# Hand-written semaphores and a TensorE hardware loop in a decode attention kernel that streams 280 MB

## The chip, the cores and the metric

The kernel runs on 1 core of one Trainium2 chip. The metric is the device time of one execution in microseconds (us), median of several. The profile is one execution taken by the hardware profiler; its span is about 1.8 us shorter than the time.

## The reference

One decode step. Attention reads a long K and V cache (2 x 8 x 32768 x 128 each, bf16, 134 MB each); a small MLP gates the result.

```python
# Both parts get xn = layernorm(A_x) as their x.
B, Sq, D = 2, 1, 512
Hq, Hkv, Sk, Dh = 32, 8, 32768, 128
# A: attention with cached K and V; rep = Hq // Hkv = 4 query heads share one K/V head
q = (x @ wq) per head
scores = einsum("bhqd,bhkd->bhqk", q, k) * Dh ** -0.5
o = einsum("bhqk,bhkd->bhqd", softmax(scores), v)
s = o.reshape(B, Sq, Hq * Dh) @ wo
# B: with S = 1 its shifted part is zero, so it is x + gelu(layernorm(x) @ w3) @ w4
g = silu(B(xn))
return A_x + s * g          # xn = layernorm(A_x)
```

## The kernel before

There are 16 groups (2 batch rows x 8 K/V heads). A group loads 8.4 MB of K and 8.4 MB of V, each as one transfer over 128 partitions. VectorE transposes K in 16 pieces, TensorE makes the scores, ScalarE exponentiates, VectorE transposes the probabilities, TensorE multiplies with V. Everything is in tile pools, and a scheduling layer puts in the semaphores.

```python
pers  = ctx.enter_context(tc.tile_pool(name="pers", bufs=1))
rings = ctx.enter_context(tc.tile_pool(name="rings", bufs=1))
...
kbuf = rings.tile([128, 3 * SLOT], BF16, name="kbuf")     # SLOT: 32 KB per partition
vbuf = rings.tile([128, 2 * SLOT], BF16, name="vbuf")
...
def emit_k(m, h, first):
    ...
    for r in range(NR):                                   # NR = 8
        T = ktp.tile([128, W], I32, tag="T", name="T")
        nc.vector.transpose(out=T[...], in_=kt[:, r * W:(r + 1) * W]...)
        for nb in range(NB):
            for e in range(2):
                nc.tensor.matmul(sc[:, :], lhsT=z[...], rhs=Tb[:, nb, :, e], ...)
    # exp on ScalarE, transpose of the result on VectorE
...
for m in range(NG):                                       # NG = 16, written out
    eps = [emit_k(m, hs[0], True)]
    if not last:
        load_k(*groups[m + 1], (m + 1) % 2, 2 if m == NG - 2 else 1)
    eps.append(emit_k(m, hs[1], False))
    for i in range(NPART):
        emit_v(m, hs[i], i, eps[i])
    if not last:
        load_v(*groups[m + 1], 2 if m == NG - 2 else 1)
    if m == NG - 2:
        # wo, in three pieces, into the free part of kbuf
```

The tail after the last loads is a chain: the last half of V lands, 32 matmuls finish o, ScalarE copies it out, eight small matmuls reduce it (oT), VectorE normalizes and spreads it (on, xm, oX), 128 matmuls multiply with wo, two VectorE operations combine with the gate, and two small transfers write the output.

The softmax here doesn't subtract the row's maximum and nothing guards it: scores larger than these inputs give would overflow.

Of the kernel before, what the change touches and what calls it, by code (L numbers as in the profile page):

```python
# [8 lines left out]
F32 = mybir.dt.float32  # L9
BF16 = mybir.dt.bfloat16  # L10
ACT = mybir.ActivationFunctionType
ALU = mybir.AluOpType
AX = mybir.AxisListType

I32 = mybir.dt.int32

KPT = 128
# [4 lines left out]
EPS = 1e-5  # L22


@with_exitstack
def kernel(
# [14 lines left out]
    nc = tc.nc  # L41

# [19 lines left out]
    QP = 32 * (NQ - 1) + B  # L62

    pers = ctx.enter_context(tc.tile_pool(name="pers", bufs=1))
    rings = ctx.enter_context(tc.tile_pool(name="rings", bufs=1))
    ktp = ctx.enter_context(tc.tile_pool(name="ktp", bufs=T_BUFS))
    epp = ctx.enter_context(tc.tile_pool(name="epp", bufs=2))
    ptp = ctx.enter_context(tc.tile_pool(name="ptp", bufs=3))
    obp = ctx.enter_context(tc.tile_pool(name="obp", bufs=2))
    smp = ctx.enter_context(tc.tile_pool(name="smp", bufs=4))  # L70
    pro_ps = ctx.enter_context(tc.tile_pool(name="pro_ps", bufs=1, space=bass.MemoryType.PSUM))
    f_ps = ctx.enter_context(tc.tile_pool(name="f_ps", bufs=3, space=bass.MemoryType.PSUM))
    sc_ps = ctx.enter_context(tc.tile_pool(name="sc_ps", bufs=2, space=bass.MemoryType.PSUM))
    o_ps = ctx.enter_context(tc.tile_pool(name="o_ps", bufs=2, space=bass.MemoryType.PSUM))

    kbuf = rings.tile([128, 3 * SLOT], BF16, name="kbuf")
    vbuf = rings.tile([128, 2 * SLOT], BF16, name="vbuf")

    def row_view(cache, b, g):
        return cache[b, g, :, :].rearrange("(p t) d -> p (t d)", p=128)  # L80

    def load_k(b, g, base, parts=1):
        w = NPART * SLOT // parts
        src = row_view(A_k_cache, b, g)
        for c in range(parts):
            nc.sync.dma_start(
                out=kbuf[:, base * SLOT + c * w:base * SLOT + (c + 1) * w],
                in_=src[:, c * w:(c + 1) * w],
            )

    def load_v(b, g, parts=1):
        w = NPART * SLOT // parts
        src = row_view(A_v_cache, b, g)
        for c in range(parts):
            nc.sync.dma_start(out=vbuf[:, c * w:(c + 1) * w], in_=src[:, c * w:(c + 1) * w])  # L95


    x_bf = pers.tile([B, D], BF16)
    nc.scalar.dma_start(out=x_bf[:, :], in_=A_x[:, 0, :])
    wq_t = kbuf[:, 2 * SLOT:3 * SLOT]  # L100
    nc.sync.dma_start(  # L101
        out=wq_t[:, 0:DK * HD],
        in_=A_wq.rearrange("(p k) f -> p (k f)", k=DK),
    )

    x4_bf = pers.tile([128, QW], BF16)
    nc.gpsimd.memset(x4_bf[:, :], 0.0)
    for n in range(NQ):
        nc.gpsimd.dma_start(out=x4_bf[32 * n:32 * n + B, :], in_=A_x[:, 0, n * QW:(n + 1) * QW])
    groups = [(b, g) for b in range(B) for g in range(Hkv)]  # L110
    NG = len(groups)
    w34 = vbuf[:, 0:SLOT]
    W4O = DK * Fdim
    nc.sync.dma_start(out=w34[:, 0:W4O], in_=B_w3.rearrange("(p k) f -> p (k f)", k=DK))  # L114
    nc.sync.dma_start(out=w34[:, W4O:W4O + FK * D], in_=B_w4.rearrange("(p f) d -> p (f d)", f=FK))  # L115
    load_k(*groups[0], 0)


    ident = pers.tile([128, 128], BF16)
    make_identity(nc, ident[:, :])  # L120
    ones_f = pers.tile([128, 128], F32)
    nc.gpsimd.memset(ones_f[:, :], 1.0)


    sel = pers.tile([128, NB, 2, 4, 32], BF16)
    for j in range(4):
        nc.vector.tensor_copy(
            out=sel[:, :, :, j, :],
            in_=ident[:, :].rearrange("p (b w e) -> p b e w", b=NB, e=2),
        )  # L130

    sel_o = pers.tile([128, VT, rep], F32)
    nc.vector.tensor_reduce(
        out=sel_o[:, :, :],
        in_=ident[:, :].rearrange("p (j a t h) -> p a t h j", j=4, t=VT, h=rep)[:, 0, :, :, :],
        axis=AX.X, op=ALU.add,
    )
    sel_h = pers.tile([128, rep], F32)
    nc.vector.tensor_reduce(
        out=sel_h[:, :],  # L140
        in_=ident[:, :].rearrange("p (r h) -> p h r", h=rep),
        axis=AX.X, op=ALU.add,
    )

    sel_r = pers.tile([128, NQ, 4, 32], BF16)
    for j in range(4):
        nc.vector.tensor_copy(
            out=sel_r[:, :, j, :],
            in_=ident[:, :].rearrange("p (w r) -> p r w", r=NQ),
        )  # L150

    mask = pers.tile([128, NQ, rep], F32)
    for r in range(NQ):
        nc.vector.tensor_reduce(
            out=mask[:, r, :],
            in_=ident[:, :].rearrange("p (h w) -> p h w", h=rep),
            axis=AX.X, op=ALU.add,
        )

    zs = [pers.tile([128, NB, 2, ZC], BF16, name=f"z{i}") for i in range(2)]  # L160
    for z in zs:
        nc.gpsimd.memset(z[:, :, :, :], 0.0)


    xf = pers.tile([B, D], F32)
    nc.vector.tensor_copy(out=xf[:, :], in_=x_bf[:, :])

    def layernorm(dst, src, t):
        stats = pers.tile([B, nc.vector.BN_STATS_DIM], F32, name=f"stats_{t}")
        nc.vector.bn_stats(out=stats[:, :], in_=src[:, :])  # L170
        mv = pers.tile([B, nc.vector.BN_AGGR_DIM], F32, name=f"mv_{t}")
        nc.vector.bn_aggr(out=mv[:, :], in_=stats[:, :])
        rstd = pers.tile([B, 1], F32, name=f"rstd_{t}")
        nc.vector.tensor_scalar_add(out=rstd[:, :], in0=mv[:, 1:2], scalar1=EPS)
        nc.scalar.activation(out=rstd[:, :], in_=rstd[:, :], func=ACT.Sqrt)
        nc.vector.reciprocal(out=rstd[:, :], in_=rstd[:, :])
        nc.vector.tensor_scalar(
            out=dst[:, :], in0=src[:, :],
            scalar1=mv[:, 0:1], scalar2=rstd[:, 0:1],
            op0=ALU.subtract, op1=ALU.mult,  # L180
        )

    xn = pers.tile([B, D], F32)
    layernorm(xn, xf, "ln1")
    xn4 = pers.tile([128, QW], F32)
    nc.gpsimd.memset(xn4[:, :], 0.0)
    for n in range(NQ):
        nc.gpsimd.dma_start(out=xn4[32 * n:32 * n + B, :], in_=xn[:, n * QW:(n + 1) * QW])
    ln2 = pers.tile([B, D], F32)
    layernorm(ln2, xn, "ln2")  # L190
    xn_bf = pers.tile([B, D], BF16)
    nc.vector.tensor_copy(out=xn_bf[:, :], in_=xn[:, :])
    ln2_bf = pers.tile([B, D], BF16)
    nc.vector.tensor_copy(out=ln2_bf[:, :], in_=ln2[:, :])

    treg = pro_ps.tile([128, 2 * DK * B], BF16, tag="pro")
    for s, src in enumerate((xn_bf, ln2_bf)):
        for k in range(DK):
            c = (s * DK + k) * B
            nc.tensor.transpose(out=treg[:, c:c + B], in_=src[0:B, k::DK], identity=ident[0:B, 0:B])  # L200
    xT = pers.tile([128, 2 * DK, B], BF16)
    nc.vector.tensor_copy(out=xT[:, :, :], in_=treg[:, :].rearrange("p (k b) -> p k b", b=B))

    q_sb = pers.tile([128, B, Hq], BF16)

    oX = pers.tile([128, Hkv, NQ, B], BF16)
    g4 = pers.tile([128, QW], F32)
    x4 = pers.tile([128, QW], F32)
    nc.gpsimd.tensor_copy(out=x4[:, :], in_=x4_bf[:, :])

    wq3 = wq_t[:, 0:DK * HD].rearrange("p (k f) -> p k f", k=DK)
    qT_ps = pro_ps.tile([128, Hq * B], F32, tag="pro")
    for h in range(Hq):
        for k in range(DK):
            nc.tensor.matmul(  # L215
                qT_ps[:, h * B:(h + 1) * B],
                lhsT=wq3[:, k, h * Dh:(h + 1) * Dh],
                rhs=xT[:, k, :],
                start=(k == 0), stop=(k == DK - 1),
            )  # L220
    nc.vector.tensor_copy(out=q_sb[:, :, :], in_=qT_ps[:, :].rearrange("p (h b) -> p b h", b=B))

    qr_ps = pro_ps.tile([128, NB, 2, B * Hq], F32, tag="pro")
    for nb in range(NB):
        for e in range(2):
            nc.tensor.matmul(
                qr_ps[:, nb, e, :],
                lhsT=sel[:, nb, e, :, :].rearrange("p j w -> p (j w)"),
                rhs=q_sb[:, :, :].rearrange("p b h -> p (b h)"),
                start=True, stop=True,  # L230
            )
    qr = pers.tile([128, NB, 2, B, Hq], BF16)
    nc.vector.tensor_copy(  # L233
        out=qr[:, :, :, :, :].rearrange("p n e b h -> p (n e b h)"),
        in_=qr_ps[:, :, :, :].rearrange("p n e c -> p (n e c)"),
    )

    def emit_mlp():
        w3v = w34[:, 0:W4O].rearrange("p (k f) -> p k f", k=DK)
# [206 lines left out]
```

## Time and profile before

| | before |
|---|---|
| time, median (3 runs) | 660.86 us (660.72 to 660.88) |
| span of the profiled run | 658.9 us |
| bytes from HBM | 280.5 MB, 426 GB/s over the span |
| VectorE waiting for K | 150.5 us in 16 waits, 9.4 us per group |
| last half of V landed / last wo piece landed | 644.11 / 653.99 us |

The page of the kernel before, part 2: the TensorE clock that was granted and the mean busy share of the transfer engines (both in tenths of the full value), and their rate, in 40 slices of the span.

```profile
PEclk9999688786968968697886959878596877859896
DMA  9999999999999999999999999999999999999995
GB/s 367 451 426 442 435 446 439 410 443 426 439 438 435 430 435 422 447 434 423 442 427 442 438 419 434 443 434 443 414 423 446 443 442 443 410 427 428 431 421 224
```

The transfer engines are busy in 39 slices of 40. The last slice is the tail. Part 4 of the same page, the chain of work that ended last, by engine and by line, says the same in one line:

```profile
DMA 75%; DVE 14%; issue 7%; PE 3%; SPq 0%; ACT 0%; DVEq 0%
DMA kbuf<-in_A_k_cache_dram 69%; DVE T L303 14%; DMA kbuf<-in_A_wo_dram 6%; PE sc L311 2%; PE o L343 1%; PE s_ps L400 0%; ACT ep L320 0%; SPq L95 0%; DVE pt L322 0%; SPq L115 0%; SPq L392 0%; SPq L114 0%; SPq L101 0%; PE S L339 0%; DVE sg L408 0%
```

Part 5, two groups of instructions (busy time and mean ns of one, then idle time before them and what ended it):

```profile
L311 PE MATMUL sc<-T,z 128*128 128x512 bf16 x992 | 276.4, 421 | 206.3 <-DVE T L303 197.8
L303 DVE STREAM_TRANSPOSE T<-kbuf 128x1024 int32<-128x1024 int32 x256 | 291.5, 1205 | 150.5 <-DMA kbuf<-in_A_k_cache_dram 150.5
```

VectorE's transposes wait 150.5 us for K; each K load is what the group waits for, and compute has slack.

The trace also records the semaphore increments of each transfer (they are in the packed trace; no view prints them). There are sixteen per load, each with a time of its own. I read each as one of the sixteen transfer engines having landed its part; that is a reading, which the trace doesn't spell out. I call the distance from the first to the last of them the *lag* of the slowest engine. For the last half of V in the kernel before, in us after 639.54:

```
0.00 0.02 0.05 0.14 0.24 0.48 0.51 2.85 2.93 2.96 2.97 2.98 4.32 4.51 4.55 4.57
```

Which engine posted which is not in the trace. Compute starts when the sixteenth is in: it came at 644.11 us, and the first matmul of the half started at 644.15 us.

### The profile page before, as it was taken

To read this page: it belongs to the slowest core of one execution; us is meant where nothing else is said; L and a number is where in the kernel's file an instruction comes from. 1 tells how busy PE (TensorE), PEld (TensorE's weight loads), DVE (VectorE), ACT (ScalarE), POOL (GpSimd) and SP (SyncE) were. 2 spreads that over 40 slices of the span, in tenths; PEclk is the share of its full clock that TensorE was granted. 3 is DMA by queue.
4 is the path that set the end of the run, shared out by engine and by line. 5 is a ranking of instruction groups with operands and counts; after the bars stand their busy time and mean duration, and the time that the engine had idled before them with its cause. 6 is when DMAs were issued, how large, how long until landed. Compare 5 with 4: busy or idle time off the path is not lost.

```text
span 658.9 us, 6323 instructions
## 1 busy us (share of the span) xinstructions
PE 386.7 (59%) x2652; PEld 172.1 (26%) x2684; DVE 346.0 (53%) x442; ACT 50.3 (8%) x152; POOL 6.9 (1%) x20
## 2 busy tenths in 40 slices
PE   2338194673828557283764729377482946738764
PEld 2313132231313223131331313123131322313322
DVE  5147192754809265381935629183572918447560
ACT  1301001010100101000010100101010010100000
POOL 4000000000000000000000000000000000000000
PEclk9999688786968968697886959878596877859896
DMA  9999999999999999999999999999999999999995
GB/s 367 451 426 442 435 446 439 410 443 426 439 438 435 430 435 422 447 434 423 442 427 442 438 419 434 443 434 443 414 423 446 443 442 443 410 427 428 431 421 224
DMA packets 6704, 280.91 MB, mean 426 GB/s; under 512 B 906, under 2 KB 916, under 8 KB 1940
## 3 DMA queue, kind: packets, MB, share of 16 engines
q1 hardware_dynamic: 6408, 280.50, 98.6%
q8 instruction: 21, 0.34, 0.2%
q0 software_dynamic: 256, 0.01, 0.0%
q14 instruction: 7, 0.06, 0.0%
q10 hardware_dynamic: 12, 0.00, 0.0%
HBM read 280.50 MB, written 0.00 MB: 426 GB/s over the span
## 4 chain that ended last, share of the span: by engine, by line
DMA 75%; DVE 14%; issue 7%; PE 3%; SPq 0%; ACT 0%; DVEq 0%
DMA kbuf<-in_A_k_cache_dram 69%; DVE T L303 14%; DMA kbuf<-in_A_wo_dram 6%; PE sc L311 2%; PE o L343 1%; PE s_ps L400 0%; ACT ep L320 0%; SPq L95 0%; DVE pt L322 0%; SPq L115 0%; SPq L392 0%; SPq L114 0%; SPq L101 0%; PE S L339 0%; DVE sg L408 0%
## 5 line engine op out<-in xcount | busy, mean ns | idle before, releaser
L311 PE MATMUL sc<-T,z 128*128 128x512 bf16 x992 | 276.4, 421 | 206.3 <-DVE T L303 197.8
L303 DVE STREAM_TRANSPOSE T<-kbuf 128x1024 int32<-128x1024 int32 x256 | 291.5, 1205 | 150.5 <-DMA kbuf<-in_A_k_cache_dram 150.5
L311 PEld LDWEIGHTS <-z 128*128 128x128 bf16 x1024 | 105.7, 103 | 371.2 <-issue 278.7
L343 PE MATMUL o<-vbuf,pt 128*16 128x512 bf16 x1024 | 69.9, 434 | 3.2 <-DMA vbuf<-in_A_v_cache_dram 3.2
L320 ACT ACTIVATE ep<-sc 128x512 bf16<-128x512 f32 x32 | 19.1, 597 | 493.2 <-PE sc L311 451.2
L334 DVE MEMSET o<- 128x512 f32 x16 | 7.8, 485 | 69.3 <-ACT ob L352 68.3
L322 DVE STREAM_TRANSPOSE pt<-ep 128x512 bf16<-128x512 bf16 x32 | 22.6, 707 | 34.7 <-ACT ep L320 34.4
L343 PEld LDWEIGHTS <-pt 128*16 128x16 bf16 x1024 | 27.2, 99 | 37.9 <-issue 18.2
L339 PE MATMUL S<-sm,ones_f 128*128 128x4 f32 x64 | 10.7, 238 | 26.1 <-DVE sm L338 26.1
L355 PE MATMUL oT<-sel_o,ob 128*128 128x4 f32 x128 | 16.9, 255 | 11.1 <-ACT ob L352 11.1
L355 PEld LDWEIGHTS oT<-sel_o,ob 128*128 128x128 f32 x128 | 15.5, 191 | 19.3 <-ACT ob L352 19.3
L339 PEld LDWEIGHTS S<-sm,ones_f 128*128 128x128 f32 x64 | 10.7, 188 | 30.9 <-DVE sm L338 28.4
L352 ACT COPY ob<-o 128x512 f32<-128x512 f32 x16 | 9.4, 586 | 83.4 <-PE o L343 83.4
L362 DVE TENSOR_TENSOR on<-oT,rec 128x4 bf16<-128x4 f32 x16 | 2.6, 162 | 21.8 <-PE oT L355 21.8
L286 ACT COPY z<-qr 32x16 bf16<-32x16 bf16 x64 | 12.6, 198 | 11.5 <-DVE qr L233 10.9
L360 DVE RECIPROCAL rec<-S 128x4 f32<-128x4 f32 x16 | 2.9, 182 | 7.6 <-PE S L339 7.6
L365 PEld LDWEIGHTS <-sel_r 128*128 128x128 bf16 x64 | 5.2, 117 | 5.2 <-issue 5.2
L320 ACT ACTIVATION_READ_ACCUMULATOR ep<-sc 128x1 f32 x32 | 6.3, 198 | 0.2
L215 PE MATMUL qT_ps<-xT,kbuf 128*128 128x2 bf16 x128 | 3.6, 165 | 4.5 <-DMA kbuf<-in_A_wq_dram 4.5
L365 PE MATMUL xp<-on,sel_r 128*128 128x4 bf16 x64 | 3.8, 164 | 4.1 <-DVE on L362 4.1
L338 DVE TENSOR_SCALAR sm<-sel_h,rs 128x4 f32<-128x4 f32 x32 | 6.0, 188 | 0.0
L370 DVE TENSOR_TENSOR xm<-xp,mask 128x16 f32<-128x16 f32 x16 | 2.8, 174 | 5.3 <-PE xp L365 5.3
(64 smaller groups left out, 48.5 us busy)
## 6 DMA issues: line engine op xcount, KB each, us to landing
kbuf<-in_A_k_cache_dram SPq DMA_DIRECT2D x2, 4096.0 KB, 29.1
vbuf<-in_A_v_cache_dram SPq DMA_DIRECT2D x2, 4096.0 KB, 26.7
kbuf<-in_A_wq_dram SPq DMA_DIRECT2D x1, 4096.0 KB
vbuf<-in_B_w_dram SPq DMA_DIRECT2D x2, 1792.0 KB, 21.6
kbuf<-in_A_wo_dram SPq DMA_DIRECT2D x1, 2048.0 KB, 35.9
kbuf<-in_A_wo_dram SPq DMA_DIRECT2D x1, 1536.0 KB, 39.1
kbuf<-in_A_wo_dram SPq DMA_DIRECT2D x1, 512.0 KB
kbuf<-in_A_k_cache_dram SPq DMA_DIRECT2D x15, 29.4
```

The source lines that it names most:

```text
L286: nc.scalar.copy(out=z[32 * j:32 * j + 32, :, :, c:c + rep], in_=qr[32 * j:32 * j + 32, :, :, b, g * rep:(g + 1) * rep],)
L303: nc.vector.transpose(out=T[:, :].rearrange("p (b t k) -> p t b k", b=NB, t=RT), in_=kt[:, r * W:(r + 1) * W].rearrange("p (t b k) -> p t ...
L311: nc.tensor.matmul(sc[:, :], lhsT=z[:, nb, e, zc:zc + 128], rhs=Tb[:, nb, :, e], start=(r == 0 and nb == 0 and e == 0), stop=(r == NR - 1 ...
L320: nc.scalar.activation(out=ep[:, :], in_=sc[:, :], func=ACT.Exp, scale=inv_sqrt_dh, accum_out=rs[:, :])
L322: nc.vector.transpose(out=pt[:, :, :].rearrange("p r (t h) -> p t r h", h=rep), in_=ep[:, :].rearrange("p (t r h) -> p t r h", r=NR, h=rep),)
L334: nc.vector.memset(state["o"][:, :], 0.0)
L338: nc.vector.tensor_scalar_mul(out=sm[:, :], in0=sel_h[:, :], scalar1=rs[:, 0:1])
L339: nc.tensor.matmul(S[:, :], lhsT=ones_f[:, :], rhs=sm[:, :], start=(i == 0), stop=(i == NPART - 1))
L343: nc.tensor.matmul(o[32 * j:32 * j + VT * rep, :], lhsT=pt[:, r, a * VT * rep:(a + 1) * VT * rep], rhs=vt[:, u * VT:(u + 1) * VT, :].rearr ...
L352: nc.scalar.copy(out=ob[:, :], in_=o[:, :])
L355: nc.tensor.matmul(oT[:, :], lhsT=ob[:, t * Dh:(t + 1) * Dh], rhs=sel_o[:, t, :], start=(t == 0), stop=(t == VT - 1),)
L365: nc.tensor.matmul(xp[:, r, :], lhsT=sel_r[:, r, :, :].rearrange("p j w -> p (j w)"), rhs=on[:, :], start=True, stop=True,)
```

## The change

The intent: put everything in one hand-synchronized section, so that no scheduler waits are left, and turn 15 of TensorE's 16 groups into a hardware loop. The loop body is the same in each turn, so TensorE waits for a fixed value there instead of a growing count and then lowers the semaphore itself (a *take-down*, `take` below). The order of loads, the tile sizes and the arithmetic stay. The diff, cut to its core:

```diff
+def take(eng, sem, n=1):
+    eng.wait_ge(sem, n).then_inc(sem, -n)
...
-    pers = ctx.enter_context(tc.tile_pool(name="pers", bufs=1))
-    rings = ctx.enter_context(tc.tile_pool(name="rings", bufs=1))
-    # ... nine more pools ...
-    kbuf = rings.tile([128, 3 * SLOT], BF16, name="kbuf")
-    vbuf = rings.tile([128, 2 * SLOT], BF16, name="vbuf")
+    pers = ctx.enter_context(tc.tile_pool(name="pers", bufs=1))
+    psum = ctx.enter_context(tc.tile_pool(name="psum", bufs=1, space=bass.MemoryType.PSUM))
+    kbuf = pers.tile([128, 3 * SLOT], BF16, name="kbuf")     # now the first tile of the pool
+    vbuf = pers.tile([128, 2 * SLOT], BF16, name="vbuf")
+    Ts = [pers.tile([128, RT * NB * 32], I32, name=f"T{i}") for i in range(T_BUFS)]
...
+    with tc.tile_critical():
...
+        for m in range(1, NG):                       # SyncE
+            wait(sp, (p_t, NT * (m - 1) + NR)); load_k(m)
+            wait(sp, (p_o, m));                 load_v(m)
...
+        def scores():
+            take(pe, s_z)
+            for i in range(NPART):
+                for r in range(NR):
+                    take(pe, s_t)
+                    # four matmuls
+                    last_mm.then_inc(p_t.sem, 1)
...
+        with pe.Fori(0, last):
+            scores()
+            values(lambda h: take(pe, s_v, 16) if h == 0 else None)
+        scores()
+        values(lambda h: wait(pe, (d_vl[h], 16)))
```

VectorE, ScalarE and SyncE stay written out. Small things also moved: x is loaded by ScalarE's queue four times after a memset, eight small GpSimd transfers are gone, z has one buffer, and the reciprocal of the softmax sum now comes after the oT matmuls.

## The prediction

> **What bounds the kernel now.** Transfers do. The page gives a mean DMA share of 90% or more in 39 of 40 slices and 426 GB/s over the span; the chain of waits is 75% DMA. One group's 16.8 MB of K and V take 38.6 us (transfers of K land at 119.6, 158.2, 197.2 us). The compute of a group is shorter: VectorE transposes (1.2 us each, 16 per group) and TensorE leave VectorE idle for K 150.5 us in 16 waits (groups view), 9.4 us per group. Each K load is issued 29 us, each V load 32 us before landing, so the queue never runs empty. Only the start and the end are open: the first transfer is issued at 0.74 us, the last two pieces of wo land at 652.7 and 653.9 us, the span ends at 658.9 us.
>
> **A second-order effect that the change touches.** The trace shows the 16 engines' increments of each large transfer. They land within 0.6 us of each other at 10 us, but within 2.0 us at 60 us, 3.1 us at 310 us and 4.5 us at the last wo pieces, in steps of about 1.45 us: for the second wo piece seven engines within 0.5 us, then five at 2.8 to 3.0, four at 4.2 to 4.5. Meanwhile the queue of instruction fetches has 21 packets of 16 KiB (page, part 3), 0.9 us each. I read each fetch as delaying one DMA engine by about 1.45 us; the slowest engine, with three, sets every landing. [...] 21 blocks is about TensorE's unrolled stream (2652 matmuls, 2684 weight loads).
>
> **What the change does.** Same work, tiles, loads and order of loads. Removed: the scheduler's waits, one buffer of z, a third pt, 15 of 16 memsets of o (0.49 us each, off the path), eight small GpSimd transfers. Added: a few dozen waits, some 20 take-downs per group on TensorE, a loop-back branch; the first x loads wait for a memset and queue behind wq, so layer norm may come about 10 us later. In the profile of before the MLP ends at 25 us, the first K lands at 42 us, so V's first load, which waits for the MLP, still has time. None of this is on the path: about 9 us of slack per group absorbs it.
>
> TensorE's program shrinks to about 1,370 instructions, 5 to 6 blocks. If the loop body (about 300 instructions, 19 KB) stays resident, engine spread falls from 4.5 to about 1.5 to 2 us, and all late landings come 2 to 3.5 us earlier, V's last half included, so the tail moves whole. If each turn fetches its two or three pages again[...], there are 30 to 45 fetches, and the spread stays or grows by up to 3 us. I give residence 60%.
>
> **Prediction.** 658.3 us, 8 in 10 between 655.5 and 663. Faster by over 2%: 1%; within 2%: 96%; slower by over 2%: 3%.
>
> **What would show each step.** Instruction packets on the queue of TensorE: 5 to 7 (resident) or over 30. Spread of the 16 landings at the last wo piece: about 1.5 us or 4.5 and more. DMA rate in the middle unchanged (about 430 GB/s); VectorE still idle for K about 9 us per group; tail from last wo landing to end still about 5 us.
>
> **What would make it wrong.** x landing so late that the first V load comes after 40 us; a loop-back stall over 9 us; a costly entry or exit of the hand-made section; or transfers bounded by something shared, so that spread costs nothing (then within 1 us of before).

From the page before, as an estimate: 21 packets of 16 KiB on q8 for 2652 matmuls and 2684 weight loads are about 254 instructions per packet, or 64.5 bytes each, if q8 carries TensorE's program (a1 tests that). 1,370 instructions are then 5.4 packets. The forecast's sum: it came to 660.8 us less about 2.5 us for earlier landings, 658.3 us. The 60% for residence were my estimate.

## More of the kernel before

Part 3, the queues (packets, MB, share of the time of 16 engines):

```profile
q1 hardware_dynamic: 6408, 280.50, 98.6%
q8 instruction: 21, 0.34, 0.2%
...
q14 instruction: 7, 0.06, 0.0%
```

q1 carries the loads. q8 and q14 carry instructions: 21 packets of 16 KiB on q8 and, within the loads, six packets of 8 KiB on q14.

The tail of the kernel before in the timeline view (start us, duration us, engine, line, operation, output<-inputs, count, and in brackets the idle time before it and what ended it):

```profile
644.15 3.38 PE L343 MATMUL o<-vbuf,pt 128*16 128x512 bf16 x32 [3.18 <-DMA vbuf<-in_A_v_cache_dram]
...
647.58 0.59 ACT L352 COPY ob<-o 128x512 f32<-128x512 f32 x1 [9.74 <-PE o L343]
...
648.22 1.05 PE L355 MATMUL oT<-sel_o,ob 128*128 128x4 f32 x8 [0.69 <-ACT ob L352]
...
649.32 0.16 DVE L362 TENSOR_TENSOR on<-oT,rec 128x4 bf16<-128x4 f32 x1 [9.96 <-PE oT L355]
...
649.70 1.09 PE L400 MATMUL s_ps<-kbuf,oX 128*2 128x128 bf16 x64
...
650.01 0.17 DVE L372 TENSOR_REDUCE oX<-xm 128x4 bf16<-128x16 f32 x1
652.79 1.88 PE L400 MATMUL s_ps<-kbuf,oX 128*2 128x128 bf16 x64 [2.00 <-DMA kbuf<-in_A_wo_dram]
...
655.43 0.66 SPq L412 DMA_DIRECT2D out_dram<-out  x1
```

And the same stretch by windows (us of each engine's busy time, number of instructions, then granted clock, transfer share, GB/s):

```profile
644.00:648.00 4.00, 3.38 (x32) 1.03 (x31) 0.00 (x0) 0.42 (x1) 0.00 (x0) 0.60 1.04 426
648.00:652.00 4.00, 2.31 (x76) 2.06 (x77) 0.51 (x3) 0.17 (x1) 0.00 (x0) 0.83 0.71 288
652.00:656.00 4.00, 1.88 (x64) 1.58 (x63) 0.58 (x2) 0.00 (x0) 0.00 (x0) 0.50 0.14 55
```

Here the first 64 wo matmuls start at 649.70 us, before the last oX is done, and the others then wait for the second and third piece of wo (652.74 and 653.99 us), so the landing of wo ends the kernel.

## The result and the profile after

| | before | after |
|---|---|---|
| time, median (4 runs each) | 660.79 us | 661.22 us (660.88 to 661.54) |
| ratio | | 1.0006, 95% interval 0.9992 to 1.0020 |
| span of the profiled run | 658.9 us | 659.8 us |
| instruction packets on q8 | 21 | 5 |
| VectorE waiting for K | 150.5 us | 150.5 us |
| last half of V landed: first engine / last | 639.54 / 644.11 us | 640.80 / 644.96 us |
| last wo piece landed | 653.99 us | 654.98 us |

A ratio is the mean time of one kernel's runs over that of the other's of the same rounds, so it is not quite the ratio of the medians quoted. Executions over 1.5% slower than the fastest of the same kernel are left out of the means.

The page after, parts 2 and 3:

```profile
DMA  8999999999999999999999999999999999999994
GB/s 366 434 443 441 434 445 421 421 445 433 441 442 405 441 434 441 441 445 401 441 433 445 441 413 429 438 441 441 441 401 445 433 445 437 417 429 430 421 421 197
```

```profile
q1 hardware_dynamic: 6408, 280.50, 98.5%
q8 instruction: 5, 0.08, 0.1%
q14 instruction: 6, 0.05, 0.0%
```

The loop does what it was meant to do: q8 falls from 21 to 5 packets. The body, an estimated 300 instructions from counting the source, or 19 KB at 64.5 bytes each (the estimate from the page before, given beside the prediction), is fetched once and then stays for 15 turns: the packets start at 28.4, 35.4, 69.3, 641.1 and 653.7 us, none in between. Yet the loads don't end earlier. The chain view of after:

```profile
PE 1%; DVE 0%; issue 0%
PE bank L540 1%; DVE sg L547 0%; DVE out L549 0%; PE bank L519 0%; DVE xm L470 0%; DVE oX L473 0%
```

It stops after 12 pieces, at the first take-down. The groups say what happened to it:

```profile
L486 PE MATMUL bank<-T,z 128*128 128x512 bf16 x1024 | 283.1, 428 | 184.7 <-PEq L45 179.6
L449 DVE STREAM_TRANSPOSE T<-kbuf 128x1024 int32<-128x1024 int32 x256 | 290.6, 1206 | 150.5 <-DMA kbuf<-in_A_k_cache_dram 150.5
```

TensorE's waits are now put down to "PEq L45", its own sequencer at the helper `take`, which lowers the semaphore itself. The 1% is a limit of the view and no finding. VectorE still waits 150.5 us for K, so the middle of the kernel is bound as before. The tail of after:

```profile
645.00 3.59 PE L503 MATMUL bank<-vbuf,pt 128*16 128x512 bf16 x32 [5.08 <-DMA vbuf<-in_A_v_cache_dram]
...
648.65 0.59 ACT L431 COPY ob<-bank 128x512 f32<-128x512 f32 x1 [12.14 <-PE bank L503]
...
649.38 1.84 PE L513 MATMUL bank<-sel_o,ob 128*128 128x4 f32 x8 [0.78 <-PEq L45]
...
651.47 0.16 DVE L468 TENSOR_TENSOR on<-bank,rec 128x4 bf16<-128x4 f32 x1
...
652.27 0.17 DVE L473 TENSOR_REDUCE oX<-xm 128x4 bf16<-128x16 f32 x1
...
652.50 3.58 PE L540 MATMUL bank<-kbuf,oX 128*2 128x128 bf16 x128 [0.47 <-DVE oX L473]
...
656.77 0.65 SPq L553 DMA_DIRECT2D out_dram<-out  x1
```

```profile
644.00:648.00 4.00, 3.00 (x32) 0.98 (x32) 0.00 (x0) 0.00 (x0) 0.00 (x0) 0.50 1.02 407
648.00:652.00 4.00, 2.65 (x20) 1.97 (x12) 0.34 (x2) 0.59 (x1) 0.00 (x0) 0.50 0.78 310
652.00:656.00 4.00, 3.53 (x129) 3.29 (x128) 0.35 (x2) 0.00 (x0) 0.00 (x0) 0.50 0.06 22
```

Three things differ. The last half of V lands 0.85 us later; its first engine is 1.26 us later, of which 0.21 us were there from the start, since the first transfer is issued at 0.95 instead of 0.74 us. TensorE runs the rest at a granted clock of 0.50: the oT matmuls take 1.84 us instead of 1.05. The clock records show that it fell to 0.50 during the wait for V in both kernels, at 643.78 us before and 642.99 us after, but came back at 647.19 us before and not until 656.65 us after. The idle wait was 5.1 us after and 3.2 us before; that this decided it was not tested. And the hand-written section has one wait of its own here: all 128 wo matmuls wait for the last oX and run in one go from 652.50 to 656.08 us, where the first 64 used to start ahead of it. The output transfer is issued at 656.77 instead of 655.43 us. The close after the output's landing is some 0.5 us shorter, so that 0.9 us is left in these two spans.

The lag tells why the landing didn't profit. For four loads of the changed kernel, the five latest of the sixteen engines, in us after the first one:

```
first at 214.85   0.90 1.22 1.56 1.68 1.73
first at 234.21   0.89 1.54 1.65 1.71 2.16
first at 427.75   0.89 1.51 1.62 1.69 3.11
first at 601.93   0.88 1.49 1.59 1.65 4.12
```

One engine goes from 1.22 to 2.16 to 3.11 to 4.12 us while the others stand still. Its steps fall at the q14 packets of 232.5, 424.6 and 604.6 us. A packet at 47.7 us seems to have made the 1.22, which first shows in the next load. These are spaced by about 185 us; VectorE has an estimated 29 instructions per group in the built program, so 8 KiB (127 instructions at the same estimate of 64.5 bytes) last about 4.4 groups of 38.7 us, 170 us. So I took them for VectorE's program, all fetched by the same transfer engine. The fifth packet within the loads, at 188.0 us, moved another engine (to 0.90 us). The experiments test the reading.

### The profile page after: what moved, and what is told of

The parts are those of the page before. It is cut to its first block, busy times and chain, and to the rows that moved or that the text cites. A ratio compares the mean times of both kernels' runs of the same rounds, so it can differ in the third digit from the quotient of the medians.

```text
span 659.8 us, 6521 instructions
## 1 busy us (share of the span) xinstructions
PE 393.7 (60%) x2684; PEld 165.5 (25%) x2684; DVE 337.0 (51%) x428; ACT 50.3 (8%) x152; POOL 5.7 (1%) x18
## 5 line engine op out<-in xcount | busy, mean ns | idle before, releaser
L486 PE MATMUL bank<-T,z 128*128 128x512 bf16 x1024 | 283.1, 428 | 184.7 <-PEq L45 179.6
L449 DVE STREAM_TRANSPOSE T<-kbuf 128x1024 int32<-128x1024 int32 x256 | 290.6, 1206 | 150.5 <-DMA kbuf<-in_A_k_cache_dram 150.5
L486 PEld LDWEIGHTS bank<-T,z 128*128 128x128 bf16 x1024 | 99.3, 104 | 362.0 <-issue 283.6
L503 PE MATMUL bank<-vbuf,pt 128*16 128x512 bf16 x1024 | 68.2, 426 | 5.1 <-DMA vbuf<-in_A_v_cache_dram 5.1
L423 ACT ACTIVATE ep<-bank 128x512 bf16<-128x512 f32 x32 | 19.1, 598 | 482.2 <-PE bank L486 482.2
L503 PEld LDWEIGHTS bank<-vbuf,pt 128*16 128x16 bf16 x1024 | 26.4, 98 | 38.8 <-issue 12.6
L496 PE MATMUL bank<-sm,ones_f 128*128 128x4 f32 x64 | 9.4, 252 | 27.6 <-PEq L45 27.6
L513 PE MATMUL bank<-sel_o,ob 128*128 128x4 f32 x128 | 17.2, 258 | 12.5 <-PEq L45 12.5
L513 PEld LDWEIGHTS bank<-sel_o,ob 128*128 128x128 f32 x128 | 16.3, 199 | 20.5 <-issue 20.5
L496 PEld LDWEIGHTS bank<-sm,ones_f 128*128 128x128 f32 x64 | 8.5, 192 | 35.4 <-issue 35.4
L431 ACT COPY ob<-bank 128x512 f32<-128x512 f32 x16 | 9.4, 586 | 87.6 <-PE bank L503 87.6
```

What stands on the lines that cost most here:

```text
L423: act.activation(out=eps_[i][:, :], in_=sc[i][:, :], func=ACT.Exp, scale=inv_sqrt_dh, accum_out=rss[NPART * (m % 2) + i][:, :],)
L431: act.copy(out=ob[:, :], in_=o[:, :]).then_inc(s_ob, 1)
L449: dve.transpose(out=Ts[n % T_BUFS][:, :].rearrange("p (b t k) -> p t b k", b=NB, t=RT), in_=kt[:, r * W:(r + 1) * W].rearrange("p (t b k) ...
L486: last_mm = pe.matmul(sc[i][:, :], lhsT=z[:, nb, e, zc:zc + 128], rhs=Tb[:, nb, :, e], start=(r == 0 and nb == 0 and e == 0), stop=(r == N ...
L496: pe.matmul(S, lhsT=ones_f[:, :], rhs=sms[h][:, :], start=(h == 0), stop=(h == NPART - 1))
L503: last_mm = pe.matmul(o[32 * j:32 * j + VT * rep, :], lhsT=pts[h][:, r, a * VT * rep:(a + 1) * VT * rep], rhs=vt[:, u * VT:(u + 1) * VT, : ...
```

## The experiments

Theory L: a packet of instructions delays the one transfer engine that fetches it; the engine that lags most sets each landing; VectorE's packets all hit the same one. Rivals: only the bytes count (the engines share one limit), or the take-downs and waits cost time. From the first four runs came theory A: the start address of the K and V buffers sets the pace of all engines.

All runs gave right results. They came in three batches on three chips (a on chip 4, b on 6, c on 14), each with the kernel before beside it: 660.76, 660.79 and 660.84 us, so times of different batches can be compared to about 0.1 us. Times are medians of 5 runs; "V" is the last half of V in the profiled run; the pace is the mean time from one load of 8.4 MB to the next at which the first of the sixteen engines lands, over the 29 steps between 40 and 602 us.

| run | time us | ratio to before | packets: q8 in all / q14 within the loads | pace us | V: first, last, lag us |
|---|---|---|---|---|---|
| before | 660.8 | 1 | 21 / 6 | 19.328 | 639.54, 644.11, 4.57 |
| after, again (a0) | 661.20 | 1.0008 | 5 / 5 | 19.353 | 640.70, 644.83, 4.13 |
| a1 loop written out | 662.43 | 1.0020 | 22 / 5 | 19.354 | 640.67, 645.87, 5.20 |
| a2 more VectorE instructions | 664.49 | 1.0057 | 5 / 8 | 19.353 | 641.39, 647.73, 6.33 |
| a3 TensorE kept warm | 661.13 | 1.0006 | 5 / 5 | 19.352 | 640.59, 644.91, 4.31 |
| b1 buffers at multiples of 512 | 659.25 | 0.9975 | 5 / 5 | 19.334 | 639.86, 643.30, 3.44 |
| b2 VectorE in a loop | 659.79 | 0.9981 | 5 / 3 | 19.350 | 640.73, 642.91, 2.18 |
| b3 = b1 + b2 | 658.65 | 0.9961 | 5 / 3 | 19.333 | 639.85, 641.64, 1.79 |
| b4 before, shifted by 128 bytes | 662.46 | 1.0026 | 21 / 6 | 19.351 | 640.52, 645.53, 5.01 |
| c1 = b3 + TensorE kept warm | 657.59 | 0.9949 | 5 / 3 | 19.326 | 639.62, 641.80, 2.18 |
| c2 = a1 + b1 | 660.41 | 0.9996 | 22 / 5 | 19.324 | 639.60, 644.17, 4.58 |
| c3 buffers at 256 past 512 | 659.15 | 0.9976 | 5 / 5 | 19.321 | 639.51, 643.31, 3.79 |
| c4 only K and V moved | 659.64 | 0.9983 | 5 / 5 | 19.320 | 639.54, 643.19, 3.65 |

The intervals of the ratios are about 0.0014 either way; runs of one kernel agree within 1.3 us or better. Pace and landings of the four a runs are from the profile taken first. The traces kept of them are of a second execution of each, with V at 640.67 and 644.85 us (lag 4.18) for a0, 640.63 and 645.64 (5.01) for a1, 642.30 and 648.05 (5.75) for a2, 640.76 and 644.62 (3.87) for a3: the last landing repeats within 0.35 us, the lag within 0.6 us.

In the kept traces one can add up, from load to load, by how much the sixteen engines together fall behind the steady pace. In a1 it is 1.44 to 1.64 us for most loads with one 16 KiB packet and under 0.15 us for each load without a packet; in a0 it is 0.9 to 1.2 us at each of VectorE's packets. So each packet costs about one engine its own delay, and the others keep their pace.

### a0_again: the changed kernel once more

No edit.

> The changed kernel once more, unedited, as the yardstick for the runs beside it. Both theories: 660.9 to 661.5 us, ratio to the kernel before 1.000 to 1.001. Its four pages of VectorE instructions should again step up the lag of one and the same transfer engine by about 1 us each, to about 4 us in the last transfers; if the lag at the end varies from 4 us by more than 0.5 us between executions, the reading of single traces is too fine.

661.20 us (660.80 to 661.58), lag 4.13 us with steps at the same packets. This profiled execution has a span of 659.0 us against 659.8 above. Its tail was luckier: there TensorE idled 2.98 us instead of 5.08 before the last half of V and its oT matmuls took 1.03 us. In the second execution the span was 659.7 us, the idle wait 5.05 us and oT took 1.84 us, as in the profile above. So the changed kernel varies by some 0.8 us by itself, and single spans of it can't settle less; the lag is steadier (4.13, 4.16 and 4.18 us in three executions; 4.31 and 3.87 us in a3, which differs in the last group alone).

### a1_unrolled: the loop written out

```diff
-        with pe.Fori(0, last):
+        for m in range(last):
             scores()
             values(lambda h: take(pe, s_v, 16) if h == 0 else None)
```

> The 15 turns of the TensorE loop written out; semaphores and take-downs as in the changed kernel. Theory L (lag: a page of instructions delays the one transfer engine that fetches it, and the engine that lags most sets each landing; VectorE's pages all hit one engine): instruction packets on TensorE's queue go from 5 back to about 20, several more engines lag by 1.5 to 4.5 us, but the worst lag stays at 4 to 5 us because one engine has VectorE's pages anyway. Mean landing of the last K piece later by 0.3 to 0.7 us, last landing within 1 us, time within 0.7 us of the changed kernel. Rival R (the take-downs and the loop itself cost time on TensorE, about 0.4 us in all): unrolling saves a loop branch per turn and the time falls to that of the kernel before or below. Rival as in my prediction (TensorE's pages set the end): unrolled 2 us slower than the changed kernel.

The queues of this run:

```profile
q8 instruction: 22, 0.36, 0.2%
q14 instruction: 6, 0.05, 0.0%
```

The time rises by 1.2 us (1.0 us by the means; the slowest run of a0 and the fastest of a1 touch). That is more than the 0.7 us that I had expected and less than the 2 us of my prediction. So the loop is a gain, and the rival "the loop and the take-downs cost time" falls for the loop. The expected size was wrong: I had the mean landing 0.3 to 0.7 us later, and for the last K piece it was 633.39 against 631.77 us, 1.6 us. That is what 17 more packets of 1.5 us on one engine each make if nothing is given back: 17 x 1.5 / 16 = 1.6 us. The first engine's pace is the same with many late neighbours (19.354 us) as with few (19.353 us), so an engine that isn't delayed gains nothing from the others' delay. That speaks against one shared limit.

### a2_dve_pad: more VectorE instructions

```diff
+            if m < last - 1:
+                for c in range(30):
+                    dve.memset(pad[:, c:c + 1], 0.0)
```

> 30 one-column VectorE memsets are added after each of groups 0 to 13, where VectorE is idle for about 9 us; nothing waits for them. They double VectorE's instruction stream. Theory L: VectorE's pages go from 4 to about 7 or 8, the lag of one transfer engine at the end goes from 4 us to 7 to 8.5 us, V's last half and wo land 3 to 4 us later, the time goes up by 2.5 to 4.5 us. Rival B (only the bytes count: transfers share one limit, 32 KB more are 0.08 us): the time moves by less than 0.3 us. Rival C (VectorE's own time counts): 30 times 0.06 to 0.1 us in 14 groups would be up to 40 us if it were on the path; I expect none of it.

```profile
q8 instruction: 5, 0.08, 0.0%
q14 instruction: 9, 0.07, 0.0%
```

Three more packets of 8 KiB within the loads (the page's ninth came after the output), the lag rises from 4.13 to 6.33 us, the last half of V lands 2.9 us later, and the time rises by 3.3 us. 24 KB at the loads' own rate are 0.06 us. The rival "only bytes count" falls; theory L stands. The landing is three times 0.97 us later, the step of the changed kernel. The lag grew by less, 2.2 us, because the first engine, too, came 0.7 us later. The kept trace suggests why: the lag rises by about 1 us a packet to 6.05 us; from then on K lands, and is used, so late that the next K load is issued only 0.9 to 2.2 us before the first engine is through with the load ahead (4.4 to 5.4 us in the changed kernel), and just there the first engine slips, by 0.3, 0.3 and 0.8 us. It seems to run out of work; this was not tested. VectorE's packets come about every 90 us here instead of every 185 us, as expected of about twice the instructions.

### a3_warm: TensorE kept warm

```diff
+                if h == 1:                         # shortened; in the last group only
+                    for _ in range(18):
+                        pe.matmul(treg_b[:, :], lhsT=z[:, 0, 0, 0:128], rhs=Ts[0]..., start=True, stop=True)
                 v_ready(h)
```

> 18 matmuls of 512 columns into an unused bank while TensorE waits 5 us for the last half of V in the last group, so that its clock stays up; results unused. If the tail of the changed kernel is bound by the chain after V's last half at half clock (granted clock 0.50 there), the second half of the o matmuls falls from 3.6 to about 1.9 us, the oT matmuls from 1.8 to about 1.0 us, the wo matmuls then wait for the last wo pieces, and the time falls by 0.5 to 1.0 us, no more, because wo lands at 655.0 us anyway. If the tail is bound by the landings alone, no change (under 0.2 us).

The tail of this run:

```profile
644.95 1.90 PE L507 MATMUL bank<-vbuf,pt 128*16 128x512 bf16 x32 [1.04 <-DMA vbuf<-in_A_v_cache_dram]
...
647.63 1.03 PE L517 MATMUL bank<-sel_o,ob 128*128 128x4 f32 x8 [0.78 <-PEq L45]
...
653.77 1.88 PE L544 MATMUL bank<-kbuf,oX 128*2 128x128 bf16 x64 [1.74 <-DMA kbuf<-in_A_wo_dram]
655.70 0.29 DVE L551 TENSOR_TENSOR sg<-bank,g 98x128 f32<-98x128 f32 x1 [5.82 <-PE bank L544]
```

o and oT take 1.90 and 1.03 us, as expected, instead of 3.59 and 1.84 us in the changed kernel's profile, where the granted clock was 0.50; by these times the clock stays up. The time doesn't follow: 661.13 against 661.20 us, only the spread of the runs shrinks (661.07 to 661.24). The wo matmuls wait for the last pieces (653.73 and 654.97 us) and the gate follows at 655.70. The expected 0.5 to 1.0 us was a miss: the median doesn't move, so in the typical execution the landing ends the kernel, and the slow chain of the profile above only costs where it lasts longer than that. This is inferred from the medians; of the three profiles taken of the unedited changed kernel, two had the slow chain.

### b1_aligned: buffers at multiples of 512 bytes

```diff
+    pers.tile([128, 96], F32, name="shift")
     kbuf = pers.tile([128, 3 * SLOT], BF16, name="kbuf")
```

> The changed kernel with 384 unused bytes per partition ahead of the K buffer. The K and V buffers then start at multiples of 512 bytes, as in the kernel before, not at 128 bytes past one; all later tiles move with them. In the traces so far the transfer engine that is first at each load needs 19.353 us per 8.4 MB load in all kernels written by hand, unrolled or not, and 19.328 us in the kernel before. Theory A (the start address of the destination): 19.328 us here, hence 0.8 us less over the 33 loads' worth of data (0.025 us times 33), landings and time 0.6 to 0.9 us earlier than the unedited changed kernel (661.2). Rival T (the pace comes from the waits or the order of issue in the hand-written section): 19.353 us and no change of time.

659.25 us, 1.95 us less, and faster than the kernel before. The pace falls to 19.334 us. The gain is twice what I had sized: the first engine has the last half of V 0.84 us earlier (639.86 against 640.70), and the lag is 0.69 us smaller besides (3.44 against 4.13). The median 64 KiB packet of the loads took 2418 ns here and in the kernel before, 2421 to 2422 ns in the changed kernel. Over all runs it is 2418 ns in each of the seven kernels with K and V at multiples of 256 bytes and 2420 to 2422 ns in each of the seven without.

### b2_dve_loop: VectorE in a loop

VectorE's groups 0 to 13 become seven turns of two groups. The core of the edit:

```diff
-        for m in range(NG):
-            ...  wait(dve, (p_t, n + 1 - T_BUFS))         # T's buffer is free again
+        dve.memset(rec[:, :], 0.0).then_inc(s_f, 3)       # three free buffers to begin with
+        def dve_group(m, out_ap, is_last=False):
+            ...  if r != 4: take(dve, s_f)                # raised by TensorE for r = 0 to 6
+        with dve.Fori(0, (NG - 2) // 2) as it:
+            for par in range(2):
+                dve_group(par, oX2[:, bass.ds(it * 2 + par, 1), :]...)
+        for m in range(NG - 2, NG):
+            dve_group(m, ...)
```

> The changed kernel with VectorE's groups 0 to 13 as seven turns of a hardware loop of two groups each, on semaphores that VectorE takes down itself; T's buffers are released by a semaphore of their own, oX is written at an address made from the loop's index. Theory L (the pages of VectorE's program all delay one transfer engine): VectorE's pages at about 230, 425 and 605 us go, the worst lag at the last loads falls from 4.1 to 1.7 to 2.3 us, V's last half lands near 642.8 us, the time falls by 1.5 to 2.3 us to about 659.2 us. If VectorE fetches a page again in each turn, the lag and the time grow instead by 1 us per fetch. If the lag of one engine is not what sets the end, the time stays at 661.2 us (or grows with the take-downs).

```profile
q8 instruction: 5, 0.08, 0.0%
q14 instruction: 4, 0.03, 0.0%
```

The packets of about 230, 425 and 605 us are gone; the loads see three (52.5, 190.4 and 617.1 us). The lag falls to 2.18 us, the last half of V lands at 642.91 us, the time falls by 1.4 us to 659.79 us (659.2 expected). So those packets were VectorE's, and with a2, which adds VectorE instructions and touches no wait, this shows that they set the end. (b2 alone would not: it also changes VectorE's semaphores.) VectorE's loop, too, is not fetched again in each turn.

### b3_both: both edits

> Both edits: buffers moved to multiples of 512 bytes and VectorE in a loop. Theories A and L together: the gains add, 2.3 to 3.1 us below the unedited changed kernel, about 658.4 us, faster than both kernels. If only one theory holds, that one's gain alone.

658.65 us, 2.55 us below the changed kernel and clearly below both kernels. The gains don't add in full (1.95 + 1.4 would be 3.4). The tail shows what took over:

```profile
641.68 3.59 PE L510 MATMUL bank<-vbuf,pt 128*16 128x512 bf16 x32 [2.88 <-DMA vbuf<-in_A_v_cache_dram]
...
646.05 1.84 PE L520 MATMUL bank<-sel_o,ob 128*128 128x4 f32 x8 [0.78 <-PEq L45]
...
649.62 3.58 PE L547 MATMUL bank<-kbuf,oX 128*2 128x128 bf16 x128 [0.70 <-DVE oX L472]
653.26 0.29 DVE L554 TENSOR_TENSOR sg<-bank,g 98x128 f32<-98x128 f32 x1 [3.69 <-PE bank L547]
```

The last wo piece lands at 651.37 us, but TensorE is busy with wo from 649.62 to 653.20 us, at half clock by its times (o 3.59, oT 1.84, wo 3.58 us, as in the changed kernel at a granted 0.50): the chain after V ends the kernel now.

The clock records of the kernels before and after, but for the last of each, have lengths of 3.41 us or multiples of it. In b3 the clock fell at 636.64 us after 3.41 us in which TensorE was busy for 1.57 us, and the second half of o then took 3.59 us although the wait just before it was only 2.88 us. In the changed kernel the 3.41 us before the fall at 642.99 us held 0.35 us of work. What makes the clock fall was not tested.

### b4_before_shifted: the kernel before, shifted

```diff
+    rings.tile([128, 32], F32, name="shift")
     kbuf = rings.tile([128, 3 * SLOT], BF16, name="kbuf")
```

> The kernel before with 128 unused bytes per partition ahead of its K buffer, so that K and V start 128 bytes past a multiple of 512, as in the changed kernel; nothing else is edited. Theory A: the first engine's pace goes from 19.328 to 19.353 us per load, the time up by 0.6 to 0.9 us, to about 661.6 us. Rival T: no change, 660.8 us.

662.46 us, up by 1.7 us; pace 19.351 us; lag 5.01 instead of 4.57 us. Theory A holds in the other kernel too, where no wait was touched. As in b1 the size is about double of the pace alone.

### c1_both_warm: both edits and a warm TensorE

The edits of b3, and the 18 matmuls of a3 cut to 10.

> The kernel with both edits (buffers at multiples of 512 bytes, VectorE in a loop; 658.65 us) and 10 unused matmuls on TensorE while it waits for the last half of V. There the last wo piece landed at 651.37 us but the wo matmuls ran on until 653.2 us at half clock, so the tail is bound by the chain after V, not by a landing. If so, the second half of o falls from 3.6 to 1.9 us, oT from 1.8 to 1.0 us, and the time by 0.9 to 1.3 us, to about 657.5 us: here the matmuls should pay, where they paid nothing in the changed kernel, whose wo pieces landed later. If the clock of the tail is no limit here either: no change.

```profile
641.85 1.90 PE L514 MATMUL bank<-vbuf,pt 128*16 128x512 bf16 x32 [2.40 <-DMA vbuf<-in_A_v_cache_dram]
...
644.53 1.03 PE L524 MATMUL bank<-sel_o,ob 128*128 128x4 f32 x8 [0.78 <-PEq L45]
...
650.46 1.88 PE L551 MATMUL bank<-kbuf,oX 128*2 128x128 bf16 x64 [1.55 <-DMA kbuf<-in_A_wo_dram]
652.39 0.29 DVE L558 TENSOR_TENSOR sg<-bank,g 98x128 f32<-98x128 f32 x1 [5.17 <-PE bank L551]
```

657.59 us, 1.06 us less than b3, as expected, and the best of all: 0.5% below the kernel before. By the means it is 0.8 us, since two of b3's five runs (657.65 and 657.85 us) were about as fast without the matmuls; the clearer sign is in the tail, where o and oT take 1.90 and 1.03 us instead of 3.59 and 1.84 (the granted clock was 1.00 from 638 to 646 us). The same edit paid nothing in a3: it pays where the chain after V, and not the landing of wo, comes last. Here the wo pieces (650.42 and 651.66 us) are last again.

### c2_aligned_unrolled: what the hand-written synchronization is worth alone

The edits of a1 and b1.

> The changed kernel with the loop written out and the buffers at multiples of 512 bytes: what is left of the change is the hand-written synchronization alone. If start address (1.7 to 1.9 us) and loop (1.2 us) explain the whole difference, 662.4 less 1.8 is 660.6 us, within 0.4 us of the kernel before. If the hand-written section costs time of its own, 661.2 us and more.

660.41 us, ratio 0.9996 (0.9982 to 1.0010). Without the loop and with the old alignment, no difference between the hand-written section and the scheduler's is seen; the interval is 0.9 us either way.

### c3_at_256 and c4_kv_only: how much alignment, and of what

c3 shifts by 128 bytes instead of 384. c4 shifts K and V as b1 does, and puts 128 more bytes behind V, so that all other tiles stand 128 bytes past a multiple of 512 as in the changed kernel.

> The changed kernel with 128 unused bytes ahead of the K buffer: K and V start at a multiple of 256 bytes that is no multiple of 512. If 256 bytes are the unit, the first engine's pace is 19.33 us per load and the time 659.3 to 659.9 us, as with 512. If 512 are needed: 19.353 us and 661.2 us.

> K and V at multiples of 512 bytes as in the aligned kernel, but every tile behind them 128 bytes past a multiple of 512, as in the unedited changed kernel. If the transfers' destinations are what matters, 659.3 to 659.9 us and a pace of 19.33 us; if it is the addresses of the tiles that the engines read and write, 661.2 us and 19.353 us.

659.15 and 659.64 us, with paces of 19.321 and 19.320 us: with K and V 256 bytes past a multiple of 512 (c3) the kernel is as fast as at a multiple of 512 (b1, 659.25 us), and the destinations of the loads are what matters (c4). The median 64 KiB packets took 0.1 to 0.2% longer in the kernels whose K and V stand 128 bytes past a multiple of 256 (2420 to 2422 against 2418 ns). The effect is shown; why such a start costs time is not.

## Why the prediction was right or wrong

The prediction said 658.3 us (655.5 to 663.0), within 2%. Measured: 661.22 us. Range held; the centre, 2.5 us faster, did not come, and two steps of it failed. That the range held is partly luck: it was 7.5 us wide, and a loss and a gain nearly cancelled. The sign that the prediction gave for a shared limit ("then within 1 us of before") came true for another reason: a1, a2 and b2 show that the spread does cost time.

- **"Transfers bound the kernel."** Right: the loads fill nearly all slices, and VectorE waits 150.5 us for K before and after.
- **"None of this is on the path: about 9 us of slack per group absorbs it."** Right for the waits and the take-downs: c2 can't be told from the kernel before. The branch is not in c2, but with it VectorE waits as long for K as before, and without it (a1) the kernel is slower. Layer norm came about 11 us later (x landed at 13.55 us) and V's first load was issued at 32.45 instead of 25.05 us, before K had landed at 42.4 us, as predicted.
- **"If the loop body stays resident ... 5 to 6 blocks."** Right: 5 packets. Neither loop was fetched again in each turn: q8 has no packet between 69.3 and 641.1 us in the changed kernel, through 15 turns of TensorE's loop, and in b2, with VectorE's of seven turns, the loads see three packets on q14 (52.5, 190.4 and 617.1 us). When a body is fetched again was not tested.
- **"I read each fetch as delaying one DMA engine by about 1.45 us."** Right in kind and near in size for TensorE's 16 KiB (steps of about 1.3 to 1.6 us); an 8 KiB packet of VectorE's puts its engine back by 0.9 to 1.0 us.
- **"Engine spread falls from 4.5 to about 1.5 to 2 us." Failed step.** It stayed at 4.1 us (4.0 us at the last wo piece, where I had named 1.5). I had charged the whole lag to TensorE's queue and overlooked the six packets on the other one. VectorE's all delay the same engine, as far as the steps show, and one engine with four of them is about as late (4.12 us) as one with three of TensorE's (4.57 us in the kernel before). Removing TensorE's 17 helped the mean landing by 1.6 us and the last landing by 1.0 us (a0 against a1; the mean is of the last K piece, the last landing of V), the time by 1.2 us. With VectorE's packets gone as well (b2), the lag is 2.2 us, what I had promised.
- **"DMA rate in the middle unchanged." Failed step.** It fell by 0.13%, too little to see in the GB/s of the page (426 and 425), but 33 loads long, 0.8 us in all. What I had listed as the same ("same work, tiles, loads") was not: the buffer's start address, a side effect of the new order of tiles, costs 1.7 us (b4) to 1.95 us (b1), more than the loop wins. The pace explains about half of that; the rest is 0.2 us that b4 has lost at the first K load already (40.49 instead of 40.31 us) and a larger lag, whose reason is open.
- **"The tail moves whole."** Half right: it depends on which comes last. In the profiled run V moved 0.85 us the wrong way, and with the clock at 0.50 the chain after V, and not the landing of wo, came last.

The sum: 660.8 us, plus 1.7 for the start address (b4), less 1.2 for the loop (a1 against a0), less 0.4 for the rest (c2 against before, inside the noise), makes 660.9; measured 661.2 us. When the changed kernel stood still, a loss of nearly 2 us hid a gain of over 1 us.

Open: which transfer engine fetches whose program can't be read from the trace; that VectorE's packets always meet the same one is inferred from the steps of the lag. Why a 16 KiB packet costs its engine 1.5 us, when a 64 KiB packet of the loads takes 2.42 us, was not tested. How many of the 0.5 to 0.7 us of smaller lag in aligned kernels belong to each packet was not separated.

## What to carry to other kernels

When transfers bound a kernel, look at the sixteen increments of a load and not only at its last one: a spread that grows in steps is a reason to look for something small that single transfer engines fetch. Here it was the program itself, and loops on TensorE and VectorE ended most of the growth (the lag was 4.57 us before, 4.13 us with the first loop and 2.18 us with both). Check the start address of each streamed buffer after any change of the order of tiles; a multiple of 256 bytes was worth 1.7 to 1.95 us of 661 here. Filling TensorE's idle wait before the final chain kept its clock up here (a3, c1: the second half of o in 1.90 instead of 3.59 us), but it pays only where that chain, and not a landing, comes last.
